# Two down products of a fused attention and two-layer MLP kernel move one stage later

## The chip, the cores and the metric

The kernel runs on one core of a Trainium2 chip. The metric is device time in microseconds (us), the median of several executions. A separate execution is recorded by the hardware profiler; all rows below come from that one.

The engines of the core run side by side, each through its own list of instructions in a fixed order: TensorE (PE in the rows, with its weight loads as PEld), VectorE (DVE), ScalarE (ACT), GpSimd (POOL) and the queue that issues most transfers (SP).

## What is computed

```python
def reference(q, k, v, moe_*, moe2_*):           # cut
    scores = (q @ k.T) / 8 + bias                # 4 batches, 8 heads, 576 positions, 64 wide
    attn   = softmax(scores where 0 <= i - j < 128)
    x = (attn @ v)  as 2304 tokens x 512
    h = max(max(x @ w1, x @ w2), x @ w3)         # 512 -> 768, three weights
    x = h @ w_out                                # 768 -> 512
    g = x @ w_gate                               # 512 -> 1536
    return (g * sigmoid(g) * (x @ w_val)) @ moe2_w_out
```

All of it is in float32. The kernel keeps the precision by splitting an operand into a rounded head and the remainder, and makes three matmuls (head by head, head by remainder, remainder by head) for each product of the two layers.

## The kernel before

**Sub-chunks and stages.** The tokens of each of the 4 batches are cut into a sub-chunk of 256 and one of 320 positions. `order` lists the eight sub-chunks, (0,0), (0,1), (1,0) and so on to (3,1). Each goes through three steps.

- *Attention* of a sub-chunk runs over 4 pairs of heads. A pair has 2 blocks of queries in the first sub-chunk and 3 in the second, so there are 8 or 12 units. A unit makes scores (L295, L296), a softmax on DVE and ACT, a transpose on PE (L336), a copy and a masked select into the tile `t` (L348, L352), the product with the values on PE (L374), three small steps that add its parts (L378 on ACT, L379 and L381 on DVE), and a split of the result into the tile `x` on POOL (L80, L77). The tile for the product with the values has one buffer and `t` has two. The steps are staggered: those of the values stand four units behind those of the scores.
- *The up product* (`up_groups`, matmuls at L111 to L113 named `ps<-x,w`) has 18 pieces: 6 columns of the hidden layer by 3 weights, 12 matmuls each. A piece needs one PSUM bank of the four in `ps_m`. Its matmuls go over the four pairs of heads in turn, so the last three need the last pair. ACT copies the first weight's result (L152), DVE takes the maximum (L154) and POOL splits it into `h`.
- *The down product* (`down_groups`, named `ps<-h,wo`) has 3 pieces of 36, 18 and 18 matmuls. Its results go through a tile `y` with two buffers (ACT L181, DVE L77) and are stored to DRAM (L183).

A matmul of these products has 256 columns for the first sub-chunk of a batch and 320 for the second. `x` of each size has one buffer.

**The second layer** follows (`second`). Its 36 weight tiles are loaded (L120) into four raw buffers and converted (`prep_w`: ACT L90, DVE L93, L94, L96, ACT L99, DVE L77 into `u`). The raw buffers and the pool of the first 12 converted tiles lie where the pools of the attention lay, and so wait for its end. The other tiles take the places of the first layer's weights as those fall free. `gate` makes 24 matmuls of 512 columns named `pg<-y,u` (L111 to L113), and ACT (L516), DVE (L517, L518) and POOL (L80, L77 named `a`) turn them into `a`. `down` makes 12 matmuls named `po<-u,a` (L531 to L533). The token chunks of 512 have 12 such rounds each, and during the first one the weights are still being converted.

**The order of work.** `spread(main, others, early)` writes out the program: it sets the steps of the attention evenly between the pieces of `main`, so that the last one stands `early` pieces ahead of the end. The program's order is only a priority. `tc.high_priority(100)` makes an instruction 100 places more urgent, and the context is opened with `schedule_with_timeline_sim=True`: a planner runs through the kernel with its own costs, gives each engine the most urgent instruction that its costs call ready, and so fixes the order in which each engine then works on the chip. In this plan work may overtake other work that is not ready.

From sub-chunk 3 on, stage `i` is the loop at L570: the down product of sub-chunk `i-1` and the up product of sub-chunk `i` are the main pieces (21), and the attention of sub-chunk `i+1` is spread over all but `EARLY` = 3 of them. The last turn of the loop is i = 6. Then the pools of the attention are closed, and L580 and L581 make the down product of (3,0), the up product of (3,1) and its down product, with the first conversions spread between them.

Of the kernel before, what the change touches and what calls it, by code (L numbers as in the profile page):

```python
# [34 lines left out]
HIGH, EARLY = 100, 3  # L35
# [4 lines left out]
NORM0, K0 = "pp", 4  # L40
AH = 0, 100
A1, E1 = 3, 0
YAT = 8
LN, LT, LV = 1, 2, 4

# [5 lines left out]
def kernel(ctx: ExitStack, tc, q0, k0, q1, k1, qk0, qk1, vv, w123, wo1, wgv, wo2, out):  # L51
# [24 lines left out]
    def low(eng, out, raw, head):  # L76
        eng.tensor_tensor(out=out, in0=raw, in1=head.bitcast(F32), op=ALU.subtract)  # L77

    def pool_round(out, in_):
        nc.gpsimd.tensor_scalar(out=out, in0=in_, scalar1=1.0, scalar2=1.0, op0=ALU.mult, op1=ALU.mult)  # L80
# [27 lines left out]
    def mm3(ps, wt, col, xt_h, xt_l, first, last):  # L108

        wh, wl = wt[:, 0, col:col + P], wt[:, 1, col:col + P]  # L110
        nc.tensor.matmul(ps, wh, xt_h, start=first, stop=False)  # L111
        nc.tensor.matmul(ps, wh, xt_l, start=False, stop=False)  # L112
        nc.tensor.matmul(ps, wl, xt_h, start=False, stop=last)  # L113
# [25 lines left out]
    def up_groups(b, s):  # L139

        n = SUBS[s][1]
        m = {}

        def group(f, e):
            xt = x_t[b, s]
            ps = ps_m.tile([P, 512], F32, tag="m", name="ps1")
            for k in range(KD):
                mm3(ps[:, :n], w1[f, e], k * P, xt[k][:, 0, :n], xt[k][:, 1, :n], k == 0, k == KD - 1)
            with tc.high_priority(HIGH):
                if e == 0:  # L150
                    m[f] = tmp.tile([P, 320], F32, tag="m0", name="m0")
                    nc.scalar.copy(m[f][:, :n], ps[:, :n])  # L152
                else:
                    nc.vector.tensor_tensor(out=m[f][:, :n], in0=ps[:, :n], in1=m[f][:, :n], op=ALU.max)  # L154
                if e == 2:
                    ht = hp.tile([P, 2, n], F32R, tag=f"h{s}", name=f"h{s}", bufs=NF1)
                    pool_round(ht[:, 0, :], m[f][:, :n])
                    low(nc.gpsimd, ht[:, 1, :], m[f][:, :n], ht[:, 0, :])
                    hs[b, s, f] = ht

        return [lambda f=f, e=e: group(f, e) for f in range(NF1) for e in range(3)]

    def down_groups(b, s):
        t0, n = SUBS[s]
        t0 += b * S

        def part(ps, d, ks):
            for k in ks:
                ht = hs[b, s, k]
                mm3(ps[:, :n], wo[k], d * P, ht[:, 0, :], ht[:, 1, :], k == 0, k == NF1 - 1)  # L170

        def group(ds):

            ps = [ps_m.tile([P, 512], F32, tag="m", name="ps2") for d in ds]
            for i, d in enumerate(ds):
                part(ps[i], d, range(NF1 - 1))
            for i, d in enumerate(ds):
                part(ps[i], d, [NF1 - 1])
                with tc.high_priority(HIGH):
                    y = tmp.tile([P, 2, 320], F32R, tag="y", name="y")  # L180
                    nc.scalar.copy(y[:, 0, :n], ps[i][:, :n])  # L181
                    low(nc.vector, y[:, 1, :n], ps[i][:, :n], y[:, 0, :n])
                nc.sync.dma_start(  # L183
                    out=y_dram[:, d * P:(d + 1) * P, t0:t0 + n].rearrange("a p n -> p a n"),
                    in_=y[:, :, :n].bitcast(F32),
                )

        return [lambda ds=ds: group(ds) for ds in ((0, 1), (2,), (3,))]

    order = [(b, s) for b in range(B) for s in range(2)]  # L190
# [242 lines left out]
    for t in range(len(units) + LV):  # L433
# [9 lines left out]
        if t < len(units):  # L443
            u = units[t]
            if u.j == BLOCKS[u.s][0]:
                i = todo.index((u.b, u.s, u.p))
# [6 lines left out]
    def attn_units(i):  # L453
        return steps[done_at[i]:done_at[i + 1]]

    def spread(main, *others, early=0):


        done = [0] * len(others)
        for i, g in enumerate(main):  # L460
            for n, o in enumerate(others):
                while done[n] < len(o) and done[n] * (len(main) - early) <= i * len(o):
                    o[done[n]]()
                    done[n] += 1
            g()
        for n, o in enumerate(others):
            for piece in o[done[n]:]:
                piece()
# [98 lines left out]
    spread(up_groups(0, 1), conv_o, a2[:len(a2) * A2 // 8])  # L567
    spread(down_groups(0, 0) + down_groups(0, 1), a2[len(a2) * A2 // 8:] + a3[:len(a3) * A3 // 8])
    spread(up_groups(*order[2]), a3[len(a3) * A3 // 8:], early=EARLY)
    for i in range(3, len(order) - 1):  # L570
        spread(down_groups(*order[i - 1]) + up_groups(*order[i]), attn_units(i + 1), early=EARLY)
    for g in down_groups(*order[-2])[:D6]:
        g()
    actx.close()
# [12 lines left out]
    for n, (c, f) in enumerate(blocks):  # L587
        if c == 0:
            for piece in conv[C3 + 3 + 3 * f:C3 + 6 + 3 * f]:
                piece()  # L590
        if f == YAT and c + 1 < len(CHUNKS):
            load_y(c + 1)
# [60 lines left out]
```

## Time and profile before

| | |
|---|---|
| median of 3 executions | 912.55 us (912.53 to 913.21) |
| profiled execution, its own time | 910.81 us |
| span from first to last instruction | 909.1 us |
| PE busy | 879.1 us (97%) |
| DVE, POOL, ACT busy | 490.9, 414.1 and 353.0 us |
| mean granted TensorE clock | 0.984 of full speed |

The span is what the rows cover; 1.7 us of the execution's own time lie around it. A PE that is called busy is not always at its peak pace, since its matmuls overlap: the pace is read from the distance between the starts of two matmuls, or from their count in a stretch.

### The profile page before, as it was taken

The numbers are of one execution on the slowest core, as the hardware profiler recorded it, in microseconds if no ns is written. First come the engines' busy times: TensorE is split into PE (matmuls) and PEld (weight loads), VectorE is DVE, ScalarE is ACT, GpSimd is POOL, SyncE is SP. The second block draws the span as 40 slices with busy tenths as digits, with TensorE's granted clock in tenths as the row PEclk, the third lists the DMA queues.
The fourth block names the chain that finished last, engine by engine and source line by source line (L and its number), as shares of the span: only waits on it lengthen the run. The fifth ranks groups of instructions, "written<-read, shape, count | busy, mean of one in ns | idle before, by whom it ended". The sixth has DMA issues, their size and how long they took to land.

```text
span 909.1 us, 14915 instructions
## 1 busy us (share of the span) xinstructions
PE 879.1 (97%) x5256; PEld 783.6 (86%) x5256; DVE 490.9 (54%) x1373; ACT 353.0 (39%) x988; POOL 414.1 (46%) x599
## 2 busy tenths in 40 slices
PE   8896899999999999999998999999999999999998
PEld 6675899999999999999976788888888888888897
DVE  7899987867677686647989941111111111111121
ACT  6887647756576566513444411000010001000101
POOL 5897557676777677542325522222222122221222
PEclk9997899999999999999998999999999999999999
DMA  9755224324232430125655533000210002000100
GB/s 334 256 151 168 86 70 122 115 73 141 67 111 59 131 109 28 44 83 174 220 203 170 182 93 123 17 1 0 93 47 1 1 1 93 1 1 0 47 1 23
DMA packets 40873, 82.74 MB, mean 91 GB/s; under 512 B 3680, under 2 KB 16480, under 8 KB 40800
## 3 DMA queue, kind: packets, MB, share of 16 engines
q1 hardware_dynamic: 39712, 79.71, 27.2%
q10 hardware_dynamic: 1088, 2.10, 0.7%
q8 instruction: 41, 0.67, 0.3%
q14 instruction: 32, 0.26, 0.1%
HBM read 67.63 MB, written 14.16 MB: 90 GB/s over the span
## 4 chain that ended last, share of the span: by engine, by line
PE 75%; issue 8%; DVE 7%; POOL 6%; DMA 2%; ACT 1%; ACTq 0%; SPq 0%; POOLq 0%; DVEq 0%
PE pg L113 9%; PE pg L111 9%; PE pg L112 9%; PE ps L111 9%; PE ps L112 9%; PE ps L113 9%; PE po L533 5%; PE po L531 5%; PE po L532 5%; PE pv L374 3%; POOL a L80 2%; PE pt L336 2%; DVE wf L94 1%; POOL a L77 1%; PE sc L296 1%
## 5 line engine op out<-in xcount | busy, mean ns | idle before, releaser
L80 POOL TENSOR_SCALAR a<-sg 128x512 fp32r<-128x512 f32 (+1 forms) x60 | 48.6, 810 | 330.7 <-DVE sg L518 327.3
L111 PE MATMUL pg<-y,u 128*128 128x512 f32 (+1 forms) x480 | 176.9, 369 | 1.2 <-DVE y L77 1.2
L113 PE MATMUL pg<-y,u 128*128 128x512 f32 (+1 forms) x480 | 176.8, 368 | 0.0
L112 PE MATMUL pg<-y,u 128*128 128x512 f32 (+1 forms) x480 | 176.8, 368 | 0.0
L111 PE MATMUL ps<-x,w 128*128 128x320 f32 (+1 forms) x576 | 173.3, 304 | 2.7 <-POOL x L80 1.5
L113 PE MATMUL ps<-x,w 128*128 128x256 f32 (+1 forms) x576 | 174.4, 304 | 1.3 <-DVE w L77 1.3
L112 PE MATMUL ps<-x,w 128*128 128x320 f32 (+1 forms) x576 | 173.6, 302 | 0.0
L517 DVE TENSOR_TENSOR sg<-pg,sg 128x512 f32<-128x512 f32 (+1 forms) x60 | 38.2, 637 | 249.7 <-ACT sg L516 249.7
L516 ACT ACTIVATE sg<-pg 128x512 f32<-128x512 f32 (+1 forms) x60 | 33.4, 556 | 317.2 <-PE pg L113 313.7
L111 PEld LDWEIGHTS ps<-x,w 128*128 128x128 f32 x576 | 110.5, 193 | 5.1 <-POOL x L80 2.1
L113 PEld LDWEIGHTS ps<-x,w 128*128 128x128 f32 x576 | 110.9, 193 | 3.3 <-DVE w L77 2.3
L112 PEld LDWEIGHTS ps<-x,w 128*128 128x128 f32 x576 | 110.9, 193 | 0.5 <-POOL x L80 0.2
L111 PEld LDWEIGHTS pg<-y,u 128*128 128x128 f32 x480 | 90.8, 189 | 17.0 <-DVE y L77 1.6
L112 PEld LDWEIGHTS pg<-y,u 128*128 128x128 f32 x480 | 90.6, 189 | 15.6
L113 PEld LDWEIGHTS pg<-y,u 128*128 128x128 f32 x480 | 90.6, 189 | 15.1
L352 POOL TENSOR_SCALAR_AFFINE_SELECT t<-pk 128x512 fp32r<-128x512 f32 (+3 forms) x128 | 72.9, 592 | 42.6 <-PE pv L374 20.5
L531 PE MATMUL po<-u,a 128*128 128x512 f32 x216 | 85.1, 394 | 2.2 <-POOL a L80 2.2
L533 PE MATMUL po<-u,a 128*128 128x512 f32 x216 | 84.9, 395 | 2.3 <-POOL a L77 2.3
L532 PE MATMUL po<-u,a 128*128 128x512 f32 x216 | 84.9, 393 | 0.0
L309 ACT ACTIVATE z<-z,mn 128x128 f32<-128x128 f32 (+1 forms) x160 | 63.4, 398 | 30.9 <-DVE mn L304 29.6
L77 POOL TENSOR_TENSOR a<-sg,a 128x512 fp32r<-128x512 f32 (+1 forms) x60 | 73.1, 1218 | 5.0
L518 DVE TENSOR_TENSOR sg<-pg,sg 128x512 f32<-128x512 f32 (+1 forms) x60 | 38.2, 637 | 58.5 <-PE pg L113 58.3
(83 smaller groups left out, 1707.5 us busy)
## 6 DMA issues: line engine op xcount, KB each, us to landing
wr<-wgv SPq DMA_DIRECT2D x24, 512.0 KB, 4.2
qkr<-qk SPq DMA_DIRECT2D x24, 416.0 KB, 3.5
wr<-w SPq DMA_DIRECT2D x18, 512.0 KB, 5.5
qkr<-qk SPq DMA_DIRECT2D x24, 256.0 KB, 2.8
wr<-wo SPq DMA_DIRECT2D x12, 512.0 KB, 4.7
y<-y_dram SPq DMA_DIRECT2D x12, 512.0 KB, 5.0
y_dram<-y SPq DMA_DIRECT2D x16, 320.0 KB, 2.6
out<-ob SPq DMA_DIRECT2D x18, 256.0 KB, 2.0
```

Of the source, the lines that this page charges most:

```text
L77: eng.tensor_tensor(out=out, in0=raw, in1=head.bitcast(F32), op=ALU.subtract)
L80: nc.gpsimd.tensor_scalar(out=out, in0=in_, scalar1=1.0, scalar2=1.0, op0=ALU.mult, op1=ALU.mult)
L111: nc.tensor.matmul(ps, wh, xt_h, start=first, stop=False)
L112: nc.tensor.matmul(ps, wh, xt_l, start=False, stop=False)
L113: nc.tensor.matmul(ps, wl, xt_h, start=False, stop=last)
L309: nc.scalar.activation(out=z[:m, a], in_=z[:m, a], func=AF.Exp, scale=-1.0, bias=mn[:m, a:a + 1], accum_out=sm[:m, a:a + 1],)
L352: nc.gpsimd.affine_select(out=t[:, i, :n, :, :m], in_=w[:, :n, :, :m], compare_op=op, fill=0.0, base=0, pattern=[[0, n], [0, 2], [-sign, m ...
L517: nc.vector.tensor_tensor(out=sg, in0=pair[0], in1=sg, op=ALU.mult)
L518: nc.vector.tensor_tensor(out=sg, in0=pair[1], in1=sg, op=ALU.mult)
L531: nc.tensor.matmul(po, ah, w2[f, 2][:, 0, :], start=f == 0, stop=False)
L532: nc.tensor.matmul(po, ah, w2[f, 2][:, 1, :], start=False, stop=False)
L533: nc.tensor.matmul(po, al, w2[f, 2][:, 0, :], start=False, stop=f == NF2 - 1)
```

## The change

The loop stops two stages earlier. For i = 5 the up product of (2,1) is now alone with the attention of (3,0), still with `EARLY` = 3. The next stage holds the down products of (2,0) and (2,1) and the up product of (3,0), 24 pieces, and the attention of (3,1) is spread over all but `LAST` = 9 of them. What follows is as before, and no instruction is added or removed.

```diff
+
+LAST = 9
 YAT = 8
...
-    for i in range(3, len(order) - 1):
+    for i in range(3, len(order) - 3):
         spread(down_groups(*order[i - 1]) + up_groups(*order[i]), attn_units(i + 1), early=EARLY)
+
+    i = len(order) - 3
+    spread(up_groups(*order[i]), attn_units(i + 1), early=EARLY)
+    spread(down_groups(*order[i - 1]) + down_groups(*order[i]) + up_groups(*order[i + 1]), attn_units(i + 2), early=LAST)
     for g in down_groups(*order[-2])[:D6]:
         g()
     actx.close()
```

## Rows read from the trace of the kernel before

**Rows 1.** The page: busy time of each engine and its instructions.
```profile
PE 879.1 (97%) x5256; PEld 783.6 (86%) x5256; DVE 490.9 (54%) x1373; ACT 353.0 (39%) x988; POOL 414.1 (46%) x599
```

**Rows 2.** PE's waits: first 120 to 400 us, then 380 to 560 us.
```profile
PE pt L336 <- DVE t L77: 0.3, 1, 0.3
...
PE po L533 <- POOL a L77: 2.3, 3, 0.9
PE po L531 <- POOL a L80: 2.2, 1, 2.2
PE ps L111 <- ACT m L152: 1.2, 1, 1.2
PE pg L111 <- DVE y L77: 1.2, 1, 1.2
```

**Rows 3.** Stretches of 20 us: length, busy by engine (instructions), PE clock, DMA.
```profile
400.00:420.00 20.00, 18.80 (x142) 18.53 (x142) 7.95 (x21) 5.59 (x13) 4.78 (x11) 1.00 0.59 209
420.00:440.00 20.00, 20.00 (x138) 20.00 (x138) 19.97 (x34) 9.08 (x17) 8.50 (x8) 1.00 0.49 158
440.00:460.00 20.00, 18.82 (x113) 17.34 (x112) 18.47 (x32) 9.98 (x17) 2.95 (x3) 1.00 0.79 264
...
500.00:520.00 20.00, 20.00 (x90) 16.57 (x89) 19.90 (x33) 9.21 (x15) 10.61 (x5) 1.00 0.57 180
```

**Rows 4.** The same in stretches of 5 us, around the fall of the clock.
```profile
480.00:485.00 5.00, 2.47 (x10) 1.41 (x8) 4.96 (x9) 2.15 (x4) 4.92 (x2) 0.95 0.65 197
485.00:490.00 5.00, 4.41 (x10) 3.47 (x11) 5.00 (x9) 2.11 (x5) 1.29 (x2) 0.50 0.53 175
490.00:495.00 5.00, 5.00 (x20) 4.01 (x19) 4.97 (x8) 2.84 (x5) 1.83 (x2) 0.87 0.30 77
```

**Rows 5.** Timeline, all engines, 407 to 417 us: start, duration, instruction, [idle before].
```profile
407.93 0.31 PE L111 MATMUL ps<-x,w 128*128 128x320 f32 x1
...
408.96 0.56 PE L374 MATMUL pv<-t,v 128*128 128x128 f32 x4
...
411.11 0.32 POOL L77 TENSOR_TENSOR x<-xr,x 128x64 fp32r<-128x64 f32 x1
...
411.45 0.82 SPq L120 DMA_DIRECT2D wr<-wgv  x2
...
413.66 0.75 PE L111 MATMUL ps<-x,w 128*128 128x320 f32 x4
...
415.62 0.66 ACT L90 ACTIVATE wf<-wr 128x512 f32<-128x512 f32 x1 [5.80 <-DMA wr<-wgv]
416.31 0.75 ACT L152 COPY m<-ps 128x320 f32<-128x320 f32 x2
```

**Rows 6.** Timeline of PE, 300 to 317 us.
```profile
300.73 0.28 PE L111 MATMUL ps<-h,wo 128*128 128x256 f32 x1
300.85 0.28 PE L112 MATMUL ps<-h,wo 128*128 128x256 f32 x1
...
301.33 0.63 PE L374 MATMUL pv<-t,v 128*128 128x256 f32 x4
...
311.24 0.56 PE L374 MATMUL pv<-t,v 128*128 128x128 f32 x4
311.81 0.31 PE L111 MATMUL ps<-x,w 128*128 128x320 f32 x1
...
316.84 0.75 PE L111 MATMUL ps<-x,w 128*128 128x320 f32 x4
```

**Rows 7.** Timeline of DVE, 301 to 310 us.
```profile
302.92 0.58 DVE L381 TENSOR_TENSOR xr<-pv,c 64x128 f32<-64x128 f32 x2
```

**Rows 8.** Timeline of POOL, 479 to 503 us: the split of `a`.
```profile
479.19 4.67 POOL L80 TENSOR_SCALAR a<-sg 128x512 fp32r<-128x512 f32 x1 [5.52 <-DVE sg L518]
...
489.24 0.99 POOL L80 TENSOR_SCALAR a<-sg 128x512 fp32r<-128x512 f32 x1 [3.71 <-DVE sg L518]
...
497.44 4.67 POOL L80 TENSOR_SCALAR a<-sg 128x512 fp32r<-128x512 f32 x1 [5.52 <-DVE sg L518]
```

## The prediction

> **What bounds the kernel now.** I read the page first. PE is busy for 97% of the span [rows 1], so only two things can pay: stretches in which PE stands still, and stretches in which its clock is low. The table of PE's waits says where. Between 120 and 400 us, in the stages whose order is changed, PE waits 0.3 us in all; between 380 and 560 us it waits 6.9 us (2.3, 2.2, 1.2 and 1.2) [rows 2]. The table by stretches gives the setting: from 420 us DVE is busy 19.97 of 20 us [rows 3], which is the conversion of the second layer's weights beside the first gates. The finer table shows the worst place. From 480 to 495 us PE starts 10, 10 and 20 matmuls [rows 4]; at its full pace of 90 in 20 us [rows 3], or 0.222 us each, 15 us hold 67.5. So 27.5 are missing, 6.1 us. Of these 3.1 us are PE's waits on `a` (2.2, and 0.9 of the 2.3, the longest of three), and 3.0 us are the clock, which is granted at 0.50, the lower of its two levels (1.2 against 2.4 GHz), after PE had stood still. The loss that any change around here can touch is thus 6.9 + 3.0 = 9.9 us.
>
> What starts the conversions is seen in the timeline around 411 us. The last product with the values starts on PE at 408.96, POOL's last split ends at 411.43, and 0.02 us later the first weights are asked for; ACT stands 5.80 us in its queue for them [rows 5]. The end of the attention releases everything.
>
> And the attention ends late because of the plan, not because of the chip. At 407.93 the up product of (3,1) starts, before the last values. PE makes 36 of its matmuls in four open pieces, then at 413.66 four L111 in a row [rows 5]: the plan had run out of everything that needs only the first three pairs of heads, four PSUM banks were full, and it took the heads of the last pair in all four pieces as they came. The same four stand at 316.84, after the values at 311.24 and the start of the up product of (2,1) at 311.81 [rows 6]. So in the plan the attention of the second sub-chunk of a batch is what PE waits for, each time at the start of its up product. On the chip a unit's sum is done at 303.50 after values at 301.33 [rows 6, 7], 2.2 us, and the units come 5.0 us apart (two from 301.33 to 311.24): the chip has time in hand, and these waits of the plan cost nothing there [rows 2].
>
> **The change part by part.** *The matmuls.* None is added or removed, and PE has no idle time in 120 to 400 us to win. Price 0.
>
> *The down product of (2,0)* stood between 300.73 and 311.81 [rows 6], where it filled PE while the attention of (2,1) ended. Now the up product of (2,1) is next in the program. I expect the plan to open four pieces at once, to fill the four banks with 36 matmuls and then to wait, since the down product finds no bank. The 72 matmuls come later instead, so when the attention of (3,1) ends, PE stands 72 x 0.12 us (300.73 to 300.85, [rows 6]) = 8.6 us earlier in its work: in the down product of (3,0), not in the up product of (3,1). The attention's own pace is set by its chain in the plan, not by its places in the program: its last step stands three pieces before the end of its stage, and yet its last values come after the whole down product of the next [rows 5]. So I give `LAST` and the new spacing nothing.
>
> *The wait on the first weights.* ACT's 5.80 us in front of L90 hold up L152, and PE loses 1.2 us for a bank [rows 2, 5]. Started 8.6 us earlier, this falls into the down product of (3,0), whose next piece finds other banks. I take -1.2; the bounds are -1.2 and 0.
>
> *Conversions beside the gates.* POOL's splits of `a` show DVE's pace there: 479.19 to 497.44 is 18.25 us for two gates [rows 8], where PE needs 2 x 36 x 0.222 = 16.0. DVE loses 1.1 us against PE in each gate while conversions last. Ending 8.6 us earlier they touch 8.6 / 8.0 = 1.1 gates less: -1.2 us. The lower bound is twice that, -2.4; the upper is 0, since the head start also lets DVE fall behind for longer before the first gate. The split at 479.19 takes 4.67 us, the next 0.99 [rows 8], and it is the long one that PE waits for. The Trainium skill (GPSIMD Engine Reference, 1. Specifications) says that GpSimd shares its SBUF interfaces with VectorE and contends with VectorE instructions that read two SBUF inputs; by that, fewer gates beside conversions mean fewer long splits, and the sum would keep the same sign.
>
> *The new start of the up product of (2,1).* It comes at 300.73 instead of 311.81, with three units of the last pair's attention still to come [rows 6]. PE's cover is 36 matmuls at 20 / 138 = 0.145 us [rows 3], 5.2 us, plus three products with the values at 0.56 to 0.63 us, less their overlap, an estimated 1.5: until 307.4. The chip could have the last pair's `x` at 301.33 + 2 x 2.2 + (411.43 - 408.96) = 308.2 [rows 5, 6, 7]. That is a wait of 0.8 us on PE, in front of everything, since PE takes its list in order. The bounds: 0 if more work of PE's stands in between, such as the next scores; 2.5 if in each of the three units one other step as long as DVE's 0.58 us [rows 7] goes first (0.8 + 3 x 0.58). A gain is excluded, as PE does not wait there now [rows 2]. I take 0.9, near the sum of the bare chain. Behind a waiting PE stand all later matmuls, and nothing on PE can go around it.
>
> *Two down products in a row.* They send eight results through two `y` buffers, with stores on SP between the loads for later pairs. This has a precedent: sub-chunks (0,0) and (0,1) do it within 120 to 400 us, and PE's only wait there is 0.3 us [rows 2]. Price 0, hidden by the four banks; if that cover fails, as much as the 1.2 us that a late bank costs at L152.
>
> Sum: 0 - 1.2 - 1.2 + 0.9 = -1.5 us. The profiled execution took 910.81 us (909.1 of span and 1.7 around it), so it would take 909.3; the median of the runs is 1.7 above it, and I predict 911.0. Differences below 0.2%, 1.8 us, can hardly be told from no change here.
>
> **The rivals.** *A, a wait that costs the clock (slower).* The new wait at the up product of (2,1) comes in one piece. The two waits of 1.2 us left the clock at 1.00 [rows 2, 3]; the 2.2 us on `a` was followed by 0.50 [rows 2, 4]. So this decides from a wait of about 2.2 us. At 2.5 us, with 3.0 for the clock and the gains of 2.4 kept, it gives +3.1: 915.6. For it: the last pair's chain is serial. Against it: there are three places to wait, and the chain has time in hand. The Trainium skill (TensorE: Matmul & The Clock Gate, HAM oscillation) says that a pause on PE drops the clock so that the work behind it starts cold, which is this case; rows 4 agree with 0.50.
>
> *B, the fall at 480 us goes away (much faster).* The conversions meet the gates in another phase, and no long split meets a PE that waits for it. All 6.1 us go: -1.5 - 6.1 = -7.6, 904.9. For it: of the two long splits shown only the first is followed by a fall [rows 3, 8]. Against it: DVE's shortfall per gate stays, and every second split is long.
>
> *C, nothing moves.* The plan finds a bank for the down product of (2,0) and puts it where it was. Then PE's list is the old one: 912.5, within 1 us. Against it: four open pieces in both places where the plan waits [rows 5, 6].
>
> **How the numbers follow.** The forecast gets 0.44, with its own range from -3.6 (both gains at their bounds, no new wait) to +2.5 (no gain, the longest wait, the clock kept), that is 909 to 915; A 0.22, B 0.22, C 0.12. The range of 8 in 10 reaches from B to A: 904.5 to 916.5. Faster by over 0.2%: 0.19 of the forecast, all of B, 0.01 of C: 0.42. Within: 0.20 of the forecast, 0.03 of A, 0.09 of C: 0.32. Slower: 0.05 of the forecast, 0.19 of A, 0.02 of C: 0.26.
>
> **What would show it.** The first `ps<-x,w` of 320 columns near 301 us instead of 312, with four L111 in a row some 6 us on; the last L374 some 8 us earlier and inside `ps<-h,wo` of 256 columns; the first L120 of the second layer right behind it; no wait of PE on ACT L152; the last conversion some 8 us earlier. New entries at L111, L112 or L374 in PE's waits before 315 us would be the cost. The prediction is wrong if the attention ends at the same place in PE's list (C), or if it ends earlier by much more than 8.6 us, because the spacing matters after all.

## The result, and the profile after

The changed kernel took 922.05 us (median of 4 runs, 919.34 to 922.16) against 912.88 us of the kernel before beside it: 1.0091 times as long, with an interval of 1.0073 to 1.0110. The forecast was 911.0, and its range ended at 916.5. The profiled execution took 921.96 us, with a span of 920.0. In the changed kernel's lines everything from L42 on stands 2 further down than before (L111 is L113, L374 is L376).

To see where the time went, three moments are compared in both traces: A, the first matmul behind the up product of (2,0); V, the first matmul of the up product of (3,1); and the first gate (`pg<-y,u`).

| us | before | after | difference |
|---|---|---|---|
| A | 300.73 | 303.98 | +3.25 |
| A to V | 107.20 | 114.57 | +7.37 |
| V to the first gate | 44.16 | 47.83 | +3.67 |
| first gate to the end | 457.0 | 453.6 | -3.4 |
| span | 909.1 | 920.0 | +10.9 |

Most of the 3.25 us ahead of A is not the change's. PE's list of instructions is the same until late in the up product of (2,0), at 289.67 us before and 292.43 after, so 2.76 us are already there when the lists part. The other 0.5 us is work that changed its side: the new plan puts four matmuls of scores ahead of A, so measured from the point where the lists part the loss up to V is 7.8 us and not 7.4. The profiled executions of the other orders below reach their A anywhere from 300.3 to 303.8 us, and the profiled execution of before was 2.1 us under its median. So A is the zero from here on. Two things are left: some 7.4 us were lost between A and V, and behind V a loss and a gain cancel.

The first is seen in the table of PE's waits of the changed kernel, from 300 to 330 us, and in its stretches of 4 us, with two of 2 us at the ends of the low clock and two of 1 us around its fall (length, then busy time with the number of instructions for PE, PEld, DVE, ACT and POOL, granted clock of PE, DMA share, GB/s). Before, PE waited 0.3 us in all from 120 to 400 us [rows 2].

```profile
PE pt L338 <- DVE t L79: 1.0, 1, 1.0
PE sc L297 <- DVE mn L306: 0.8, 1, 0.8
PE pv L376 <- DVE xr L383: 0.7, 1, 0.7
PE ps L114 <- POOL x L79: 0.2, 1, 0.2
```

```profile
304.00:308.00 4.00, 4.00 (x32) 4.00 (x31) 2.19 (x7) 1.07 (x3) 3.59 (x8) 1.00 0.59 156
308.00:312.00 4.00, 3.02 (x22) 2.81 (x21) 0.70 (x2) 0.74 (x2) 1.50 (x5) 1.00 0.25 92
312.00:314.00 2.00, 1.28 (x8) 1.09 (x7) 1.53 (x8) 1.21 (x5) 0.95 (x3) 0.83 0.00 0
314.00:318.00 4.00, 3.24 (x14) 2.65 (x13) 3.65 (x13) 3.95 (x13) 3.75 (x6) 0.50 0.24 66
318.00:322.00 4.00, 3.76 (x15) 3.32 (x14) 3.31 (x9) 1.74 (x5) 1.90 (x5) 0.50 0.72 214
322.00:324.00 2.00, 2.00 (x11) 2.00 (x11) 1.57 (x8) 1.93 (x8) 1.92 (x4) 0.61 0.02 7
```

```profile
312.00:313.00 1.00, 0.28 (x3) 0.09 (x1) 0.85 (x4) 0.37 (x1) 0.11 (x1) 1.00 0.00 0
313.00:314.00 1.00, 1.00 (x6) 1.00 (x7) 0.68 (x5) 0.84 (x4) 0.84 (x3) 0.65 0.00 0
```

The waits make 2.7 us. The clock stands at the lower level, 0.50 (1.2 of 2.4 GHz), from 314 to 322 us, with a partial stretch on either side. Busy time times the missing share of the clock is 1.28 x 0.17 + (3.24 + 3.76) x 0.50 + 2.00 x 0.39 = 4.5 us, an estimate. Together that is 7.2 of the 7.4. The clock falls between 313 and 314 us, behind the first two waits, of 1.0 and 0.7 us; the wait of 0.8 us that ends at 315.85 (timeline below) comes when it is low already.

What PE did there is in its timeline, with the ACT and DVE instructions that the first wait rests on and the POOL instruction that finishes the last pair's `x`:

```profile
303.98 0.31 PE L113 MATMUL ps<-x,w 128*128 128x320 f32 x1
...
307.10 0.60 PE L113 MATMUL ps<-x,w 128*128 128x320 f32 x3
...
310.03 0.31 PE L115 MATMUL ps<-x,w 128*128 128x320 f32 x1
310.18 0.63 PE L376 MATMUL pv<-t,v 128*128 128x256 f32 x4
310.90 0.37 ACT L341 CAST t<-pt 128x256 fp32r<-128x256 f32 x1 [4.48 <-PE pv L376]
...
311.30 0.42 DVE L79 TENSOR_TENSOR t<-pt,t 128x256 fp32r<-128x256 f32 x1 [3.59 <-ACT t L341]
...
311.78 0.44 PE L338 MATMUL pt<-ident,z 128*128 128x128 f32 x2 [0.98 <-DVE t L79]
312.94 0.76 PE L376 MATMUL pv<-t,v 128*128 128x128 f32 x4 [0.72 <-DVE xr L383]
...
315.85 0.58 PE L297 MATMUL sc<-r 128*128 128x256 f32 x1 [0.76 <-DVE mn L306]
...
317.39 1.44 PE L113 MATMUL ps<-x,w 128*128 128x320 f32 x4
...
318.36 0.65 POOL L79 TENSOR_TENSOR x<-xr,x 128x64 fp32r<-128x64 f32 x1
...
319.06 0.64 PE L114 MATMUL ps<-x,w 128*128 128x320 f32 x1 [0.24 <-POOL x L79]
```

From 303.98 PE makes its 36 matmuls of four open pieces, as the prediction said, and has used them up at 310.18. From there to 317.39 its list holds only steps of the attention, of (2,1) and already of (3,0): values, transposes, scores. Each needs what ACT and DVE make of the one before (PE's values at 310.18, ACT at 310.90, DVE at 311.30, PE's transposes at 311.78), and nothing stands in PE's list to fill the time. Before, the 72 matmuls of the down product of (2,0) were spread between these steps [rows 6].

The last pair's `x` is ready at 319.01, 15.0 us behind A. Before, this instruction ended about as far behind A, at 316.52 (15.8 us), with PE at work all the while:

```profile
316.20 0.32 POOL L77 TENSOR_TENSOR x<-xr,x 128x64 fp32r<-128x64 f32 x1
```

The end of the attention, in the timeline of the changed kernel:

```profile
412.95 0.56 PE L376 MATMUL pv<-t,v 128*128 128x128 f32 x4
...
415.45 0.34 SPq L122 DMA_DIRECT2D wr<-wgv  x1
...
418.55 0.31 PE L113 MATMUL ps<-x,w 128*128 128x320 f32 x1
...
420.31 0.67 ACT L92 ACTIVATE wf<-wr 128x512 f32<-128x512 f32 x1 [5.12 <-DMA wr<-wgv]
```

The last values stand 5.60 us ahead of V, inside the down product of (3,0); before, they came 1.03 us behind V [rows 5]. In PE's work the attention thus ends 6.6 us earlier. In time it does not: counted from A the last values come at 108.97 us (before 108.23), the first weights are asked for at 111.47 (before 110.72). PE has lost between A and V what the head start is made of.

Behind V, the waits of PE from 400 to 560 us, the timeline around the longest and the clock after it:

```profile
PE ps L113 <- POOL h L82: 3.5, 1, 3.5
PE po L535 <- POOL a L79: 2.8, 3, 0.9
PE po L533 <- POOL a L82: 1.8, 3, 1.0
```

```profile
449.28 0.83 POOL L82 TENSOR_SCALAR h<-m 128x320 fp32r<-128x320 f32 x1 [3.58 <-DVE m L156]
...
455.30 2.97 POOL L82 TENSOR_SCALAR h<-m 128x320 fp32r<-128x320 f32 x1 [3.91 <-DVE m L156]
...
458.33 0.70 PE L113 MATMUL ps<-h,wo 128*128 128x320 f32 x3 [3.54 <-POOL h L82]
```

```profile
460.00:464.00 4.00, 4.00 (x19) 4.00 (x18) 3.13 (x7) 1.27 (x4) 0.00 (x0) 0.57 0.95 338
...
480.00:500.00 20.00, 18.04 (x78) 14.29 (x77) 19.93 (x33) 8.80 (x14) 9.46 (x4) 1.00 0.56 181
```

In this execution the wait for ACT's L152 (now L154) is gone, and the clock does not fall between 480 and 500 us. In their place PE waits 3.54 us for the last split of `h` on POOL, which takes 2.97 us where the one before it took 0.83, and runs at a mean clock of 0.57 for 4 us, 1.7 us lost. Behind V that is 8.1 of waits and 1.7 of clock, 9.8 us; before it was 9.9.

### The profile page after: what moved, and what is told of

It is laid out like the page before. It is cut to its first block, busy times and chain, and to the rows that moved or that the text cites. A ratio compares the mean times of both kernels' runs of the same rounds, so it can differ in the third digit from the quotient of the medians.

```text
span 920.0 us, 14925 instructions
## 1 busy us (share of the span) xinstructions
PE 886.4 (96%) x5256; PEld 790.0 (86%) x5256; DVE 491.0 (53%) x1373; ACT 353.9 (38%) x988; POOL 415.5 (45%) x599
## 4 chain that ended last, share of the span: by engine, by line
PE 75%; issue 7%; POOL 7%; DVE 7%; DMA 2%; ACT 1%; SPq 0%; ACTq 0%; POOLq 0%; DVEq 0%
PE pg L113 9%; PE pg L114 9%; PE pg L115 9%; PE ps L115 9%; PE ps L114 9%; PE ps L113 9%; PE po L535 5%; PE po L533 5%; PE po L534 5%; PE pv L376 2%; POOL a L82 2%; PE pt L338 2%; DVE wf L96 1%; POOL a L79 1%; PE sc L298 1%
## 5 line engine op out<-in xcount | busy, mean ns | idle before, releaser
L115 PE MATMUL ps<-x,w 128*128 128x256 f32 (+1 forms) x576 | 176.9, 308 | 1.1 <-DVE w L79 1.1
L113 PE MATMUL ps<-x,w 128*128 128x320 f32 (+1 forms) x576 | 176.2, 309 | 1.5 <-POOL x L82 1.5
L113 PE MATMUL pg<-y,u 128*128 128x512 f32 (+1 forms) x480 | 176.5, 368 | 0.0
L114 PE MATMUL ps<-x,w 128*128 128x320 f32 (+1 forms) x576 | 175.7, 306 | 0.2 <-POOL x L79 0.2
L113 PEld LDWEIGHTS ps<-x,w 128*128 128x128 f32 x576 | 112.9, 197 | 3.8 <-POOL x L82 2.3
L115 PEld LDWEIGHTS ps<-x,w 128*128 128x128 f32 x576 | 113.1, 196 | 3.0 <-DVE w L79 1.7
L114 PEld LDWEIGHTS ps<-x,w 128*128 128x128 f32 x576 | 113.2, 197 | 1.0 <-POOL x L79 0.6
L113 PEld LDWEIGHTS pg<-y,u 128*128 128x128 f32 x480 | 90.5, 188 | 15.4
```

## The experiments

Ratios are to the kernel before, timed on the same chip beside each run (medians 912.94, 912.84 and 912.44 us in the three sets); the brackets behind a ratio hold its 95% interval. One profile was taken of each.

**The spacing alone.** Before's grouping of products, with only the last attention spread to nine pieces before the end.

```diff
-    for i in range(3, len(order) - 1):
+    for i in range(3, len(order) - 2):
         spread(down_groups(*order[i - 1]) + up_groups(*order[i]), attn_units(i + 1), early=EARLY)
+    i = len(order) - 2
+    spread(down_groups(*order[i - 1]) + up_groups(*order[i]), attn_units(i + 1), early=LAST)
```

> The grouping of before, with the attention of (3,1) spread over all but nine of its stage's 21 pieces; the down product of (2,0) stays in front of the up product of (2,1). Theory 1 (PE runs dry at the start of the up product of (2,1), because the down product that covered it is gone): no change against before, within 2 us, PE's waits between 300 and 345 us zero. Theory 2 (the denser spacing crowds DVE, ACT and POOL and costs PE its time): most of the 9 us, 6 us or more above before.

Measured: 910.6 us, 0.9982 (0.9964 to 0.9999). PE has no wait from 290 to 345 us; A to V is 107.3 us and V to the end 502.6. The spacing is not the cause of the loss.

**The spacing undone.** The changed grouping with three pieces instead of nine.

```diff
-LAST = 9
+LAST = 3
```

> The changed kernel with LAST = 3. Theory 1: still 7 to 10 us above before, with the same waits of about 2.7 us near 310 us and the clock at 0.50 behind them. Theory 2: within 3 us of before.

Measured: 918.39 us, 1.0058 (1.0032 to 1.0085). The waits near 310 us are the same or longer (1.0, 0.7, 1.2, 0.2, 0.2), the clock from 300 to 320 us is 0.84, and A to V is 113.9. The loss belongs to the grouping. Behind V this run's longest wait is 2.7 us on ACT's L154, with the attention's last values 7.2 us ahead of V: the wait that went in the changed kernel's profile is back, and longer than before the change (1.2).

**Filling the gap with idle work.** In the changed kernel the first four pieces of the up product of (2,1) make their first nine matmuls twice, so that PE has 72 matmuls of these pieces and not 36. The output is the same; 36 matmuls are added, and the planner lays the attention's steps out anew between them.

```diff
+            if (b, s) == order[5] and 3 * f + e < 4:
+                for k in range(KD - 1):
+                    mm3(ps[:, :n], w1[f, e], k * P, xt[k][:, 0, :n], xt[k][:, 1, :n], k == 0, k == KD - 2)
             for k in range(KD):
```

> The changed kernel, in which the first four pieces of the up product of (2,1) make their first nine matmuls twice; the second pass starts the sum anew. That is 36 more matmuls, 5.2 us of PE work that needs nothing PE does not have. Theory 1, with the low clock as the larger part of the loss (2.7 us of waits and 4.7 of clock): the matmuls fill the gap, no stretch at 0.50 near 315 us, and the time is about 2 us below the changed kernel. Theory 1 without the clock (only the waits are lost): about 2.5 us above the changed kernel. Theory 2 or any cause elsewhere: 5 us above.

Measured: 918.55 us, 1.0057 (1.0037 to 1.0077). Its waits from 300 to 340 us, and its stretches of 4 us:

```profile
PE pt L341 <- DVE t L79: 1.6, 1, 1.6
```

```profile
312.00:316.00 4.00, 4.00 (x31) 3.99 (x30) 1.86 (x9) 2.06 (x8) 1.65 (x4) 1.00 0.03 11
316.00:320.00 4.00, 3.52 (x27) 3.31 (x25) 3.45 (x9) 3.77 (x12) 3.39 (x6) 1.00 0.22 66
320.00:324.00 4.00, 2.84 (x20) 2.87 (x21) 3.96 (x17) 2.09 (x9) 1.03 (x3) 1.00 0.72 213
```

The clock stays at 1.00. A to V is 114.2 us: the 107.2 of before, 36 x 0.145 = 5.2 for the added matmuls, and the wait of 1.6, which makes 114.0. So the 5.2 us of matmuls of no use are paid for by what they spare, 1.1 us of waits and all of the clock's loss: PE needs work there, and pays for its lack. By the ratios the time is 3.1 us below the first measurement of the changed kernel and 1.2 below the second, which stands further down; the expectation with the clock had 2.

**A part of the product put back.** One of the three groups of the down product of (2,0) goes back ahead of the up product of (2,1); then, in a kernel of its own, two of three, with the spacing of nine.

```diff
-    spread(up_groups(*order[i]), attn_units(i + 1), early=EARLY)
-    spread(down_groups(*order[i - 1]) + down_groups(*order[i]) + up_groups(*order[i + 1]), attn_units(i + 2), early=LAST)
+    spread(down_groups(*order[i - 1])[:1] + up_groups(*order[i]), attn_units(i + 1), early=EARLY)
+    spread(down_groups(*order[i - 1])[1:] + down_groups(*order[i]) + up_groups(*order[i + 1]), attn_units(i + 2), early=LAST)
```

> The changed kernel with the first piece of the down product of (2,0), 36 of its 72 matmuls, put back in front of the up product of (2,1). Theory 1: 4.3 us of cover are back, the waits near 310 us fall below 0.5 us in all, the clock stays at 1.00, and the time is within 3 us of before. Theory 2: still 6 us or more above before.

Measured with one put back: 912.99 us, 0.9995 (0.9976 to 1.0014). Waits from 295 to 340 us, and the stretch of 300 to 320:

```profile
PE ps L114 <- POOL x L79: 0.8, 1, 0.8
PE pv L376 <- ACT r L258: 0.7, 1, 0.7
```

```profile
300.00:320.00 20.00, 18.41 (x136) 17.54 (x135) 14.12 (x48) 12.64 (x37) 13.00 (x23) 1.00 0.43 130
```

The waits are not below 0.5 us as expected: there are two of nearly the changed kernel's length, 1.5 us together. But the clock stays at 1.00, and A to V is 108.9, 1.7 above before. Why the clock holds here and not behind 1.0 and 0.7 us in the changed kernel, this run alone does not tell.

> The changed kernel with two pieces of the down product of (2,0), 54 of its 72 matmuls, back in front of the up product of (2,1); only the last piece moves. Theory 1: 6.5 us of cover are enough, no wait near 310 us, within 2.5 us of before. If theory 3 is wrong and an earlier end of the attention pays, 1 to 3 us below before.

Measured with two put back: 911.15 us, 0.9987 (0.9971 to 1.0002), no wait from 295 to 340 us, A to V 106.6. The attention's last values stand as far behind V as before (1.03 us), so this run does not test whether an earlier end pays. By the profiles, moving the last 18 of the 72 matmuls is free, moving 36 costs 1.7 us, and moving all 72 costs 7.4 (5.8 in the second profile, which follows).

**The changed kernel again**, for its size beside the runs of the second set, with no edit.

> The changed kernel once more, as the measure for the next three on one chip. 7 to 10 us above before; its trace shows 114 to 115 us from the start of the up product of (2,1) to that of (3,1), against 107 before, and again some 501 us from there to the end.

Measured: 919.83 us (915.36 to 923.0), 1.0070 (1.0045 to 1.0095). The profiled execution was the fastest of its eight runs (915.36). The waits near 310 us are the same to 0.03 us, and the clock again falls behind the first two of them. A to V is 113.0 and not the 114 to 115 expected, since the clock is low from 310.7 to 317.5 us, for 6.8 us and not 10.2. The wait for the split of `h` is 1.6 us here and not 3.5, and V to the end is 499.1 and not 501. The place before V repeats, the one behind V varies.

**Two pieces ahead of the product.** If PE's cover is what counts and not the order as such, two pieces of the up product of (2,1) can go ahead of the down product of (2,0) without loss.

```diff
-    spread(up_groups(*order[i]), attn_units(i + 1), early=EARLY)
-    spread(down_groups(*order[i - 1]) + down_groups(*order[i]) + up_groups(*order[i + 1]), attn_units(i + 2), early=LAST)
+    ups = up_groups(*order[i])
+    spread(ups[:2] + down_groups(*order[i - 1]) + ups[2:], attn_units(i + 1), early=EARLY)
+    spread(down_groups(*order[i]) + up_groups(*order[i + 1]), attn_units(i + 2), early=LAST)
```

> The down product of (2,0) follows the first two pieces of the up product of (2,1) instead of standing behind all of it; two PSUM banks are then free for it. Theory 1: the down product's matmuls run before the last values of (2,1) again, no loss near 310 us, within 2.5 us of before. Rival (an up product that starts early is the harm, whatever fills behind it): 5 us or more above before.

Measured: 909.87 us, 0.9964 (0.9945 to 0.9983). No PE wait from 295 to 340 us, A to V 106.7, and 164 matmuls from 300 to 320 us where the changed kernel makes 108:

```profile
300.00:320.00 20.00, 20.00 (x164) 19.91 (x163) 14.44 (x46) 12.22 (x36) 14.11 (x23) 1.00 0.42 126
```

> The order with two pieces of the up product of (2,1) ahead of the down product of (2,0), run again beside the kernel before for its size and as the partner of the run with h on ACT. Expected: ratio 0.995 to 0.998, no wait of PE and a clock of 1.00 from 300 to 320 us. If the first result was chance: 0.999 to 1.001.

Measured the second time: 910.69 us, 0.9986 (0.9967 to 1.0005). The profile is as expected (no wait, clock 1.00 from 300 to 320 us), the ratio is not: it is above 0.998, and its interval reaches past 1. That this order undoes the loss is shown; that it beats the kernel before is shown by one of two measurements, by 0.36%, and is within 0.2% in the other.

**What sets the loss behind V.** The changed kernel, with three of DVE's four steps in the conversion of the second layer's weights left out (L95, L96 and L98; the subtraction stays), so that these weights don't get their values.

```diff
+        if short:
+            nc.scalar.activation(out=lo.bitcast(F32), in_=hi.bitcast(F32), func=AF.Copy, scale=2.0 ** -112)
+            nc.scalar.copy(t[:, 0], lo.bitcast(F32))
+            low(nc.vector, t[:, 1], lo.bitcast(F32), t[:, 0])
+            return
...
-            prep_w(words(src, raws2, "wr2", 512), t)
+            prep_w(words(src, raws2, "wr2", 512), t, short=True)
```

> The changed kernel with the second layer's weights made by two copies on ACT and one subtraction on DVE; the three steps on DVE that join a weight's bits (L95, L96, L98) are left out, so those weights are not the reference's. Theory 3 (the head start brings nothing because what PE loses beside the conversions is set by DVE's pace there, wherever they start): PE's waits behind the start of the up product of (3,1) fall from some 8 us to under 2, the clock stays at 1.00 there, and the time falls by 7 to 11 us against the changed kernel. Rival (the loss there is POOL's own splits or the transfers): it falls by less than 3 us. The loss near 310 us stays in both.

Measured: 913.14 us, 1.0013 (0.9995 to 1.0030). That is 6.7 us below the changed kernel in the same set by the medians and 5.2 by the ratios; the theory had 7 to 11, the rival under 3. The loss between A and V stays (waits of 1.0, 0.7, 0.8 and 0.2). V to the end is 496.3 us, 5.1 less than in the first profile of the changed kernel and 2.8 less than in the second. PE's waits behind V are 3.6 us (under 2 was expected), and the clock falls once, from 470 to 473 us (none was expected), behind the longest of them, for the input of a gate:

```profile
PE pg L118 <- DVE y L79: 2.1, 1, 2.1
```

No wait on `a` is left, and from 480 us on PE is at its full pace of 90:

```profile
480.00:500.00 20.00, 20.00 (x90) 16.57 (x89) 7.69 (x12) 9.08 (x15) 4.13 (x4) 1.00 0.67 215
500.00:520.00 20.00, 20.00 (x90) 16.55 (x89) 3.46 (x5) 1.19 (x2) 5.46 (x6) 1.00 0.00 1
```

So DVE's conversions cause a large part of what PE loses behind V. How large is not settled: the two profiles of the changed kernel give 5.1 and 2.8 us, the ratios 5.2 and the medians 6.7, against an estimated 9.8 in all in the first profile.

**The split of `h` on another engine.** Did the wait of 3.5 us eat a gain? In the last sub-chunk ACT rounds `h` instead of POOL, in the changed kernel and in the order with two pieces ahead.

```diff
-                    pool_round(ht[:, 0, :], m[f][:, :n])
+                    (nc.scalar.copy if (b, s) == order[-1] else pool_round)(ht[:, 0, :], m[f][:, :n])
```

> The changed kernel, but in the up product of the last sub-chunk (3,1) the rounding of h to its first half is done by ACT instead of POOL (the subtraction that follows stays on POOL). Question: why did the 6.7 us earlier end of the attention in PE's work buy nothing behind the up product of (3,1)? Theory 5: one new wait ate it, the 3.5 us of PE on POOL's split of h (L82, 2.97 us beside the conversions) and the half pace after it, some 1.6 us; with ACT doing this step the wait is gone, the stretch from the start of the up product of (3,1) to the end falls from 501.4 to about 496.5 us, and the time is 3 to 5 us below the changed kernel's (ratio to the kernel before about 1.003). Rival: the loss is set by DVE's conversions and only changes its place, so the waits on the split of a grow in turn; the stretch stays at 499 to 502 us and the time stays within 1.5 us of the changed kernel's (ratio 1.006 to 1.010).

Measured: 915.99 us (913.5 to 920.9), 1.0048 (1.0029 to 1.0066). The wait for `h` is gone, and V to the first gate falls from 47.8 to 44.0 us; the first gate to the end rises from 453.6 to 456.6. Its waits from 462 to 570 us and the stretch of the clock:

```profile
PE po L533 <- POOL a L82: 2.2, 1, 2.2
PE po L535 <- POOL a L79: 1.6, 2, 0.9
PE pg L113 <- issue: 1.3, 1, 1.3
PE pg L113 <- DVE y L79: 1.3, 1, 1.3
```

```profile
480.00:500.00 20.00, 17.13 (x64) 12.98 (x63) 19.93 (x32) 9.12 (x15) 9.78 (x5) 0.85 0.57 166
```

In this execution the loss has gone back to the gates, with the same long wait on `a` and a fall of the clock after 480 us as before the change [rows 2, 4]; V to the end is 500.7 against 501.4. That is the rival. By the ratios the time is 2.0 us below the second measurement of the changed kernel, between the two theories (3 to 5, and under 1.5) and with intervals that overlap, and 3.9 below the first, which is within the theory. The profiled execution was also among the slowest of its runs (920.75). The size is left open.

> The order of the run with two pieces of the up product of (2,1) ahead of the down product of (2,0), with the rounding of h of the last sub-chunk on ACT instead of POOL. Theory 5: its profile showed a wait of 1.6 us on the split of h and a stretch with a clock of 0.91; both go, and it is 2 to 3 us faster than that order alone (ratio to the kernel before about 0.993 to 0.994). Rival: the loss changes its place, and the time is within 1 us of that order alone (ratio 0.995 to 0.998).

Measured: 910.0 us, 0.9970 (0.9952 to 0.9988), against 0.9986 of the same order without it: 1.5 us by the ratios, again between the two theories, and again with overlapping intervals.

## Why the prediction was wrong

**The matmuls, and the plan.** Right. None was added, and the plan did what was read from [rows 5] and [rows 6]: four open pieces, 36 matmuls, then the attention's steps.

**The down product of (2,0).** Right in kind: in PE's work the attention ends 6.6 us earlier, where 8.6 was said, and `LAST` by itself bought and cost nothing beyond 0.2%. Wrong in what follows from it: "earlier" was counted in PE's work and then spent as time. Counted from A the last values came at 109.0 us, and at 107.4 in the second profile, against 108.2 before, since it was PE that waited for the attention.

**The new start of the up product of (2,1).** This is the step that failed. It said 0.9 us, with bounds of 0 and 2.5; the trace shows 2.7 of waits and 4.5 of clock. The price of the waits came out just past its upper bound. The chain was set up as running beside PE's 36 matmuls, with the last pair's `x` done at 308.2, 7.5 us behind A; it came 15.0 us behind A. The attention's steps are in PE's list too, behind the matmuls, and go through PE, ACT and DVE in turn, so that most of the chain began only when the cover was used up; and from the last values to their `x` it took 6.1 us (312.94 to 319.01) and not the 2.5 taken from 411 us, where no further attention followed; here steps of (3,0) stand between them on ACT, DVE and POOL. And the clock was given a price only in rival A, from a wait of about 2.2 us in one piece. No single wait reached 1 us, and the clock still fell to 0.50, in the midst of 7.2 us in which PE's list held only attention steps with gaps between. Rival A named the place and the sign and the clock as the cause; its 915.6 still held both gains, which did not come, and its condition did not hold. The Trainium skill (TensorE: Matmul & The Clock Gate, HAM oscillation) also says that, in another kernel, frequent short idle times between groups of matmuls make the clock swing. This trace agrees: 0.50 behind waits of 1.0 and 0.7 us. All five profiles in which the whole product is moved with nothing put in its place have a fall between 310 and 314 us, and none of the other eight has one there, so it is shown that the order brings the fall. Which property of the stretch decides is not: putting one group back left waits of 0.8 and 0.7 us, the added matmuls one of 1.6, and both kept a clock of 1.00.

**The wait on the first weights.** The wait on L152 went in the changed kernel's profiles, as said, but an earlier end of the attention is not enough for that: with the spacing undone it ends earlier still, and the wait is 2.7 us. It bought nothing either: V to the first gate is 3.7 us longer, with 3.5 on the split of `h` in its place.

**Conversions beside the gates.** The first gate to the end took 3.4 us less (1.2 was said), and 14 of the 36 weight tiles were converted ahead of the first gate where 11 were before. That the one brings the other is not shown: the order with two pieces ahead has 12 and 452.7 us from the first gate, the changed kernel with `h` on ACT has 13 and 456.6. Ahead of the gates the conversions run beside the products of (3,1), and PE lost as much there. The prediction called DVE's 19.97 of 20 us from 420 us "beside the first gates", but the first gate starts at 452.09: it let the head start fall on work that loses nothing, and there is none, as POOL's split of `h` is exposed to DVE's conversions like that of `a`. In all executions but that with the short conversion V to the end is 498.4 to 502.6 us, whether the last values stand 7.2 us ahead of V or 1.6 behind it.

**The rivals.** B (the fall at 480 us vanishes) half happened: the fall is gone in this trace, and its 6.1 us did not come, as another took its place. C did not happen.

What stays open: why the executions differ by 3 us ahead of A in one and the same list, what makes the clock fall, how much of the loss behind V the conversions cause, and how much of the gain with `h` on ACT is real.

## What to carry to other kernels

A product that stands beside the serial end of another stage is that stage's cover. Before moving it, count what the busy engine has left until that end (here 36 matmuls, 5.2 us, as four PSUM banks allow no more), and put the steps of the serial chain that run on that engine behind the cover in the count, not beside it (here `x` came 15.0 us behind A and not 7.5). An end that comes earlier in an engine's work is earlier in time only if the engine wasn't waiting for it; and taking away one wait of a stretch that a third engine limits can move the loss along the stretch, so price the stretch (here by taking three of DVE's steps away), not the wait.

## What was not expected of the hardware

The length of the waits did not tell whether PE's clock would fall. It fell to 0.50 behind waits of 1.0 and 0.7 us in the changed kernel and stayed there until past 322 us, while one of 2.4 us in the run with 36 added matmuls (454 to 457 us) left it at 1.00. Nor did the same waits in the same place: two orders both have waits of 1.6 and 0.9 us on `a`, 0.7 us apart, and the clock falls in the run with two groups put back (first two lines) and not in the one with two pieces ahead and `h` on ACT (last two):

```profile
484.00:486.00 2.00, 1.06 (x3) 0.62 (x4) 2.00 (x3) 1.18 (x3) 1.53 (x1) 0.81 0.66 260
486.00:488.00 2.00, 2.00 (x6) 1.54 (x6) 2.00 (x5) 1.11 (x2) 0.00 (x0) 0.50 0.34 98
```

```profile
484.00:486.00 2.00, 1.06 (x5) 0.67 (x4) 2.00 (x4) 1.75 (x4) 1.15 (x1) 1.00 0.42 172
486.00:488.00 2.00, 2.00 (x10) 1.62 (x9) 2.00 (x5) 0.53 (x1) 0.00 (x0) 1.00 0.51 168
```

The same split of 128x320 on POOL took 0.46 us beside the short conversion and from 0.56 to 2.97 us beside the full one in the changed kernel. The Trainium skill (GPSIMD Engine Reference, 1. Specifications) says that GpSimd shares its SBUF interfaces with VectorE. The traces agree: the split is short beside one DVE step for a weight tile, and up to six times as long beside four.
